# An unused 96-byte tile at the far end of SBUF, and a pool taken tile by tile, in a gated linear-attention and GEGLU kernel

## The chip, the cores and the metric

The kernel runs on one core of a Trainium2 chip. The metric is the device time of one execution in microseconds. Three runs of the kernel before took 2397.22, 2397.6 and 2398.0 us; their median, 2397.6 us, is the time before.

## The reference

For one sequence of 2048 tokens with 1024 features, in float32:

```python
g = sigmoid((x * gate_w).sum(-1, keepdims=True))
q, k, v = split_heads(x @ wqkv)                    # 32 heads of 32
phi = lambda t: concat(softmax(t @ w_phi), softmax(-(t @ w_phi)))
kv, z = phi(k).T @ v, phi(k).sum(tokens)           # per head
a = merge_heads((phi(q) @ kv) / (phi(q) @ z + 1e-6)) @ wo
b = (gelu(x @ w_gate) * (x @ w_up)) @ w_down       # 3584 hidden features
return g * a + (1 - g) * b
```

## The kernel before, in words

**Arithmetic.** Each float32 operand is split into a high and a low part (`split`, or `high` on ScalarE at L509 and `low` on VectorE at L512), both of type float32r, and each product is three matmuls: high by high, high by low, low by high (`PASSES`). Nearly all matmuls have a stationary tile of 128x128 and a moving tile of 128x512.

**Three stages**, one after the other on TensorE:

1. *Keys and values* (up to about 425 us). For two halves of the heads, 16 chunks of 128 tokens each: `keys_values` (L235) issues 48 matmuls `pd<-wkv,x` for a chunk. Their stationary operand is a slice of `x`, their moving operand the folded weight `wkv`. Behind them come the 8 matmuls `pg<-f,vs` (L271) of the chunk before, which accumulate the attention state. The features (softmaxes) of a chunk are made by VectorE and ScalarE meanwhile.
2. *Gate, up and query projections* (about 425 to 1698 us). A scheme with seven block products in place of eight computes two output blocks by two token blocks in 64 units. A unit is seven products of 12 matmuls each (`product`, L854): `a<-x,wgu`, `p<-s,tyz`, `c<-x,tyz` (of the unit before), `a<-s,tyz`, `a<-s,v` (of the unit before), `c<-x,wgu`, `b<-s,tyz`. The name after the arrow lists the moving and the stationary operand: the moving ones are the quarters `x` and the sums `s1` to `s4`, the stationary ones the weight slots `wgu`, `tyz` and `v`. In some units four more matmuls `misc<-pts,kbs` (L1085) do the attention of queries. The gated results `h` go out to the DRAM tiles `lm` by DMAs that POOL issues (`spill`, L139).
3. *Output* (about 1698 us to the end). The same kind of scheme: 126 steps of 24 matmuls (L1310, into `po`). The stationary operand of a step is a left block, made anew for each step in the slots `wgu`, `wgu`, `wl` by turns; the moving operand is a right block, made from `w_down` or `wo` and used twice or more, in one of ten slots by turns: three `tyz`, then seven `tw`. Right blocks are staged in four tiles `sr` (`load_rights`, L1223); left blocks in the tiles `stage`.

**Order.** In stages 2 and 3, and for PE and DVE in stage 1 too, the order of instructions on each engine and on the SP queue is the order in which the program writes them (`manual_schedule`). An engine or the queue whose next instruction waits does nothing else.

**Where the tiles lie.** All pools take their space per partition from the two ends of SBUF. From the low end, behind 16 KiB that are reserved and four small constants, come `keep`, `ring` (with `wgu`, `stage` and the quarters `x`), and above them in turn `kp` and `kl` (stage 1), `fa` and `fp` (stage 2, with `s3`, `s4`, `h` and `kbs`) and `op` (stage 3, with `sr`, `sl`, `wl`, `tw`). From the high end down come `kw` (stage 1, with `wkv`), and later `mid` (with `tyz`) and `xa` (with `s1`, `s2`, `v`, `pts`). The four small constants end at byte 16512, and `keep` takes 512 bytes, so `ring` begins at 17024, which is 128 modulo 256; every large tile of the low end is a multiple of 512 bytes long and begins at 128 modulo 256 (and modulo 512). The high end is at 229344, 32 bytes below 224 KiB, and the tiles there are multiples of 2 KiB long, so all of them begin at 224 modulo 256 (480 modulo 512). The gap between the two ends is 352 bytes where it is least.

**How space is handed on.** The first instruction that touches a tile of a new pool waits for the old users of that space. With the default of `tile_pool` it waits until the old pools there are done with as a whole; with `reuse_waits="tile"` (already set for `mid`, `xa`, `fa` and `fp`) it waits for those old tiles alone that lay under this tile. The pool `op` has the default.

Of the kernel before, what the change touches and what calls it, by code (L numbers as in the profile page):

```python
# [8 lines left out]
F32 = mybir.dt.float32  # L9
# [7 lines left out]
P = 128  # L17
# [9 lines left out]

LAG = 4


@with_exitstack
def tile_gated_mix(ctx: ExitStack, tc: tile.TileContext, x, xT, wkT, wqT, wv, w_phi, wo,
                   w_gate, w_up, w_down, gate_w, out):
    nc = tc.nc

    keep = ctx.enter_context(tc.tile_pool(name="keep", bufs=1))
    ring = ctx.enter_context(tc.tile_pool(name="ring", bufs=2))
    psum_a = ExitStack()
    psum_d, psum_g = (psum_a.enter_context(tc.tile_pool(name=n, bufs=1, space=PSUM)) for n in ("pd", "pg"))
# [118 lines left out]
    PE, DVE, ACT, SP = (getattr(mybir.EngineType, n) for n in ("PE", "DVE", "Activation", "SP"))  # L158
# [978 lines left out]


    fours = [ctx.enter_context(tc.tile_pool(name=f"po{n}", bufs=4, space=PSUM)) for n in range(2)]
    with tc.tile_pool(name="op", bufs=1) as op, tc.manual_schedule(engines={PE, DVE, ACT, SP}):  # L1140
        acc = [ring.tile([P, 4, D], F32, name=f"x{n // 2}{n % 2}", bufs=1) for n in range(4)]
        SLOTS, MID, STAGED = N_MLP, 3, 4

# [208 lines left out]
```

## Time and profile before

| | |
|---|---|
| median of three runs | 2397.6 us |
| the profiled execution: its time, its span | 2398.33 us, 2396.5 us |
| TensorE matmul busy, x instructions | 2390.1 us, x10601 |
| VectorE, ScalarE busy | 1806.0 us, 1053.9 us |
| moved by DMA | 448.70 MB, mean 187 GB/s |
| granted TensorE clock | 1.000 |

The profiled execution was taken by the hardware profiler. Its span runs from the first to the last instruction; its time is 1.83 us longer than the span, and 0.73 us longer than the median of the runs. Busy times of one engine are not additive with those of others, since the engines run beside each other. A matmul overlaps the next: each has a duration of nearly 0.4 us by its record, but the next one starts after some 0.23 us. What counts is therefore the spacing, which is read from the start of one group of matmuls to the start of the next, by the count of the first.

### The profile page before, as it was taken

Reading aid. Unit: us, or ns where it says so; the run is one execution under the profiler, and the core shown is the slowest. Engines: PE = TensorE matmul, PEld = TensorE weight load, DVE = VectorE, ACT = ScalarE, POOL = GpSimd, SP = SyncE. Lnnn points to the kernel's source line nnn. Section 1 sums busy time; section 2 is a strip of 40 time slices with the busy share of each in tenths; the row PEclk is TensorE's granted clock in tenths of the full one; section 3 lists DMA queues with packets and bytes.
Section 4 is the critical chain, followed back from the end, with each engine's and each line's share of the span. In section 5 each row is a group of like instructions: output and inputs, shape, how many; then the busy total and the mean of one; then the engine's idle time right before and its main releaser. Section 6 shows DMA issues by size and latency. Waiting matters only on the chain.

```text
span 2396.5 us, 28304 instructions
## 1 busy us (share of the span) xinstructions
PE 2390.1 (100%) x10601; PEld 1954.6 (82%) x10601; DVE 1806.0 (75%) x2354; ACT 1053.9 (44%) x1378; POOL 170.9 (7%) x318
## 2 busy tenths in 40 slices
PE   9999999999999999999999999999999999999999
PEld 7888888888888888888888888888788888888887
DVE  7987888788788777777888778784574868867773
ACT  4323322745545444455566655554433222323221
POOL 0000010111111111110000000000000000000000
PEclk9999999999999999999999999999999999999999
DMA  8322562644444565574444444433684767977873
GB/s 301 103 73 80 195 205 97 214 162 176 159 159 164 184 205 196 178 265 136 137 151 147 133 142 151 138 128 128 237 290 166 266 223 248 333 266 272 288 263 134
DMA packets 154906, 448.70 MB, mean 187 GB/s; under 512 B 21904, under 2 KB 21904, under 8 KB 153744
## 3 DMA queue, kind: packets, MB, share of 16 engines
q1 hardware_dynamic: 124256, 346.60, 43.5%
q0 software_dynamic: 29472, 100.16, 10.9%
q8 instruction: 83, 1.36, 0.3%
q14 instruction: 55, 0.45, 0.1%
q10 hardware_dynamic: 1040, 0.13, 0.0%
HBM read 337.25 MB, written 109.58 MB: 186 GB/s over the span
## 4 chain that ended last, share of the span: by engine, by line
PE 99%; DMA 1%; DVE 0%; issue 0%; ACT 0%; SPq 0%; ACTq 0%; DVEq 0%
PE po L1310 29%; PE a L854 22%; PE c L854 15%; PE pd L235 15%; PE b L854 7%; PE p L854 7%; PE pg L271 1%; PE misc L1085 1%; PE pd L144 0%; PE pd L225 0%; DMA early<-in_wkT 0%; PE pd L545 0%; PE pg L225 0%; DMA sr<-in_w_down 0%; DMA phi_c<-in_w_phi 0%; PE pg L545 0%
## 5 line engine op out<-in xcount | busy, mean ns | idle before, releaser
L235 PE MATMUL pd<-wkv,x 128*128 128x512 f32 x1536 | 366.7, 396 | 0.0
L235 PEld LDWEIGHTS pd<-wkv,x 128*128 128x128 f32 x1536 | 285.3, 188 | 66.0 <-DVE x L44 0.3
L1310 PE MATMUL po<-tw,wgu 128*128 128x512 f32 x1344 | 310.1, 389 | 0.0
L1310 PEld LDWEIGHTS po<-tw,wgu 128*128 128x128 f32 x1344 | 252.3, 188 | 52.7
L509 ACT ACTIVATE wgu<-stage 128x1024 fp32r<-128x1024 f32 x146 | 154.3, 1057 | 236.6 <-DVE stage L1200 159.5
L512 DVE TENSOR_TENSOR wgu<-stage,wgu 128x1024 fp32r<-128x1024 f32 x146 | 178.1, 1220 | 81.3 <-ACT wgu L509 79.9
L512 DVE TENSOR_TENSOR tyz<-stage,tyz 128x1024 fp32r<-128x1024 f32 x129 | 157.0, 1217 | 63.0 <-ACT tyz L509 62.9
L854 PE MATMUL c<-x,tyz 128*128 128x512 f32 x768 | 190.0, 396 | 0.0
L854 PE MATMUL a<-s,v 128*128 128x512 f32 x768 | 189.5, 395 | 0.0
L854 PE MATMUL b<-s,tyz 128*128 128x512 f32 x756 | 187.1, 396 | 0.0
L854 PE MATMUL a<-s,tyz 128*128 128x512 f32 x768 | 185.5, 390 | 0.0
L854 PE MATMUL p<-s,tyz 128*128 128x512 f32 x756 | 184.7, 393 | 0.0
L854 PE MATMUL c<-x,wgu 128*128 128x512 f32 x756 | 183.6, 391 | 0.0
L854 PE MATMUL a<-x,wgu 128*128 128x512 f32 x756 | 182.5, 390 | 0.0
L854 PEld LDWEIGHTS c<-x,tyz 128*128 128x128 f32 x768 | 144.5, 188 | 34.2
L854 PEld LDWEIGHTS a<-s,v 128*128 128x128 f32 x768 | 144.5, 188 | 34.0
L854 PEld LDWEIGHTS a<-s,tyz 128*128 128x128 f32 x768 | 144.0, 188 | 32.1 <-DVE tyz L512 0.6
L854 PEld LDWEIGHTS b<-s,tyz 128*128 128x128 f32 x756 | 142.2, 188 | 33.9
L854 PEld LDWEIGHTS p<-s,tyz 128*128 128x128 f32 x756 | 141.9, 188 | 32.6
L854 PEld LDWEIGHTS c<-x,wgu 128*128 128x128 f32 x756 | 142.0, 188 | 32.0
L854 PEld LDWEIGHTS a<-x,wgu 128*128 128x128 f32 x756 | 141.9, 188 | 31.0
L1310 PE MATMUL po<-tyz,wgu 128*128 128x512 f32 x672 | 160.2, 396 | 0.7 <-DVE wgu L512 0.7
(199 smaller groups left out, 3460.6 us busy)
## 6 DMA issues: line engine op xcount, KB each, us to landing
stage<-lm SPq DMA_DIRECT2D x98, 512.0 KB, 4.5
sr<-in_w_down SPq DMA_DIRECT2D x84, 512.0 KB, 4.7
sl<-lm SPq DMA_DIRECT2D x70, 512.0 KB, 4.6
lm<-h POOLq DMA_DIRECT2D x112, 256.0 KB, 2.4
stage<-in_w_gate SPq DMA_DIRECT2D x43, 512.0 KB, 3.8
stage<-in_w_up SPq DMA_DIRECT2D x43, 512.0 KB, 3.7
tg<-stage POOLq DMA_DIRECT2D x28, 512.0 KB, 3.0
tu<-stage POOLq DMA_DIRECT2D x28, 512.0 KB, 2.9
```

What stands on the lines that cost most here:

```text
L235: nc.tensor.matmul(ps[m], xb[b, kc // 4][:, a, kc % 4, t * P:(t + 1) * P], w[:, e, m * 512:(m + 1) * 512], start=kc == 0 and i == 0, stop= ...
L271: nc.tensor.matmul(pkv[d // 2][:, d % 2], vs[:, d].rearrange("p a b -> p (a b)"), f[:, :, :, heads], start=first and d % 2 == 0, stop=last ...
L509: nc.scalar.activation(dst, src, AF.Copy)
L512: nc.vector.tensor_tensor(dst, src, dst_h.bitcast(F32), OP.subtract)
L854: nc.tensor.matmul(dst, w[:, h, 4 * part + kc, :], xq[:, e, kc, :], start=first and kc == 0 and i == 0, stop=kc == 3 and i == 2, skip_grou ...
L1085: nc.tensor.matmul(po[p], kbs[:, p].rearrange("p a b -> p (a b)"), pts[:, q, p, :], start=q == 0, stop=q == 1)
L1310: nc.tensor.matmul(ps[c], lefts[s][:, a, m, c * P:(c + 1) * P], made[k][:, e, m], start=d == 0 and m == 0 and n == 0, stop=d == n_duo - 1 ...
```

## The change

A new pool `edge` with one tile of 24 float32 (96 bytes per partition) is opened at the high end of SBUF before all others, and the tile is never written or read. All tiles of `kw`, `mid` and `xa` so lie 96 bytes lower: they begin at 128 modulo 256, as those of the low end do (modulo 512 they begin at 384, those of the low end at 128). And the output stage's pool `op` gets `reuse_waits="tile"`. No instruction is added, removed or moved in its engine's order by the source.

```diff
@@ -27,6 +27,8 @@
 
 LAG = 4
 
+EDGE = 24
+
 
@@ -34,6 +36,8 @@
     nc = tc.nc
 
     keep = ctx.enter_context(tc.tile_pool(name="keep", bufs=1))
+    edge = ctx.enter_context(tc.tile_pool(name="edge", bufs=1, side="right"))
+    edge.tile([P, EDGE], F32, name="edge")
     ring = ctx.enter_context(tc.tile_pool(name="ring", bufs=2))
@@ -1137,7 +1141,7 @@
 
     fours = [ctx.enter_context(tc.tile_pool(name=f"po{n}", bufs=4, space=PSUM)) for n in range(2)]
-    with tc.tile_pool(name="op", bufs=1) as op, tc.manual_schedule(engines={PE, DVE, ACT, SP}):
+    with tc.tile_pool(name="op", bufs=1, reuse_waits="tile") as op, tc.manual_schedule(engines={PE, DVE, ACT, SP}):
         acc = [ring.tile([P, 4, D], F32, name=f"x{n // 2}{n % 2}", bufs=1) for n in range(4)]
         SLOTS, MID, STAGED = N_MLP, 3, 4
```

## The prediction

> **What bounds the kernel now.** I read the page first: the busy times, the row of the granted clock and the chain that ended last.
>
> ```profile
> span 2396.5 us, 28304 instructions
> ...
> PE 2390.1 (100%) x10601; PEld 1954.6 (82%) x10601; DVE 1806.0 (75%) x2354; ACT 1053.9 (44%) x1378; POOL 170.9 (7%) x318
> ...
> PEclk9999999999999999999999999999999999999999
> ...
> PE 99%; DMA 1%; DVE 0%; issue 0%; ACT 0%; SPq 0%; ACTq 0%; DVEq 0%
> ```
>
> TensorE is busy for the whole span, its clock is granted in full in every slice, and the chain is matmuls for 99%. So the time is the number of matmuls by their spacing, and only two things can shorten it: fewer pauses or a smaller spacing. The view of waits, for TensorE alone, says how much pauses can give:
>
> ```profile
> PE pd L192 <- DVE ones L181: 1.1, 1, 1.1
> PE po L1310 <- DVE wgu L512: 0.7, 1, 0.7
> ```
>
> These are the two longest of four lines; the second is the stage boundary treated below. Pauses are thus at most 1.1 and three times 0.7 us, 3.2 in all. The spacing remains. I read it from the timeline of TensorE, as the start of one group to the start of the next, by the count of the first (columns: start, duration, line, out<-moving,stationary, count). First the output stage, where the moving operand changes between the slots `tw` (low end) and `tyz` (high end):
>
> ```profile
> 1749.47 11.04 PE L1310 MATMUL po<-tw,wgu 128*128 128x512 f32 x48
> 1760.35 5.78 PE L1310 MATMUL po<-tyz,wl 128*128 128x512 f32 x24
> 1765.96 11.08 PE L1310 MATMUL po<-tw,wgu 128*128 128x512 f32 x48
> 1776.88 5.60 PE L1310 MATMUL po<-tw,wl 128*128 128x512 f32 x24
> ```
>
> 1749.47 to 1760.35 is 10.88 us for 48 matmuls, 226.7 ns each. Then `tyz` comes: 5.61 us for 24, 233.8 ns. Then `tw` again: 10.92 us for 48. Same shapes, type, clock, line and PSUM pool; what differs is where the moving tile lies. Both `tw` and the left slots begin at 128 modulo 256; `tyz` begins at 224. The same in the projections:
>
> ```profile
> 652.19 1.10 PE L1085 MATMUL misc<-pts,kbs 128*128 128x512 f32 x4
> 653.13 2.93 PE L854 MATMUL c<-x,wgu 128*128 128x512 f32 x12
> ...
> 658.71 2.90 PE L854 MATMUL a<-x,wgu 128*128 128x512 f32 x12
> 661.44 2.93 PE L854 MATMUL p<-s,tyz 128*128 128x512 f32 x12
> 664.21 2.97 PE L854 MATMUL c<-x,tyz 128*128 128x512 f32 x12
> 667.01 2.90 PE L854 MATMUL a<-s,tyz 128*128 128x512 f32 x12
> 669.75 2.96 PE L854 MATMUL a<-s,v 128*128 128x512 f32 x12
> 672.55 2.91 PE L854 MATMUL c<-x,wgu 128*128 128x512 f32 x12
> 675.29 2.97 PE L854 MATMUL b<-s,tyz 128*128 128x512 f32 x12
> 678.10 2.89 PE L854 MATMUL a<-x,wgu 128*128 128x512 f32 x12
> ```
>
> The seven products of a unit, 12 matmuls each, take 2.73 (`a<-x,wgu`, 128 against 128), 2.77 (`p<-s,tyz`, 224 against 224), 2.80 (`c<-x,tyz`, unlike), 2.74 (`a<-s,tyz`, 224 against 224), 2.80 (`a<-s,v`, unlike), 2.74 (`c<-x,wgu`, 128 against 128) and 2.81 us (`b<-s,tyz`, unlike). 12 by 226.7 ns would be 2.72. So it isn't the place of one operand that costs, since 224 against 224 comes within 0.02 us of the floor, but that the two operands of a matmul differ modulo 256. An alike product behind an unlike one first needs some matmuls to fall into step: 2.73 to 2.77 in place of 2.72. And in the first stage:
>
> ```profile
> 109.21 11.35 PE L235 MATMUL pd<-wkv,x 128*128 128x512 f32 x48
> 120.40 1.12 PE L271 MATMUL pg<-f,vs 128*128 128x256 f32 x8
> 121.36 11.35 PE L235 MATMUL pd<-wkv,x 128*128 128x512 f32 x48
> ```
>
> 11.19 us for 48 matmuls `pd<-wkv,x` (224 against 128), 233.1 ns; then 0.96 us for the eight shorter ones.
>
> **The change part by part, and the sum.** It adds no instruction. The address shift makes the two operands of every matmul alike modulo 256, at 128. I take the spacing that like operands have in the long runs of `tw`, 226.7 ns, for all matmuls with 512 columns. The counts:
>
> ```profile
> L235 PE MATMUL pd<-wkv,x 128*128 128x512 f32 x1536 | 366.7, 396 | 0.0
> ...
> L854 PE MATMUL c<-x,tyz 128*128 128x512 f32 x768 | 190.0, 396 | 0.0
> ...
> L1310 PE MATMUL po<-tyz,wgu 128*128 128x512 f32 x672 | 160.2, 396 | 0.7 <-DVE wgu L512 0.7
> ```
>
> ```profile
> L1310 PE MATMUL po<-tyz,wl 128*128 128x512 f32 x336 | 80.8, 395 | 0.0
> ...
> L1085 PE MATMUL misc<-pts,kbs 128*128 128x512 f32 x128 | 35.1, 396 | 0.0
> ```
>
> Stage 1: 1536 matmuls are 32 chunks of 48; a chunk falls from 11.19 to 10.88 us: 32 by 0.31 is 9.9 us. Stage 2: 768 is 64 units of 12; a unit of 84 falls from 19.39 (658.71 to 678.10) to 19.04 us: 64 by 0.35 is 22.4. The 128 attention matmuls go in fours, 0.94 us for four against 0.91: 32 by 0.03 is 1.0. Stage 3: 672 and 336 are 42 steps with `tyz`, from 5.61 to 5.44: 42 by 0.17 is 7.1; and the 0.04 us of falling into step behind about 12 blocks of `tyz` steps, 0.5. Together 40.9 us, all of it on the path, since nothing else ends a wait there.
>
> The other edit is worth a pause at the stage boundary (all engines, same columns):
>
> ```profile
> 1690.11 2.97 PE L854 MATMUL b<-s,tyz 128*128 128x512 f32 x12
> ...
> 1692.92 2.97 PE L854 MATMUL a<-s,v 128*128 128x512 f32 x12
> ...
> 1695.81 1.06 ACT L509 ACTIVATE tyz<-stage 128x1024 fp32r<-128x1024 f32 x1 [1.33 <-DVE stage L1113]
> ...
> 1702.18 0.54 POOL L139 DMA_DIRECT2D lm<-h  x1 [1.91 <-DVE h L836]
> 1706.86 1.92 SPq L1223 DMA_DIRECT2D sr<-in_w_down  x4
> 1707.01 1.06 ACT L509 ACTIVATE wl<-stage 128x1024 fp32r<-128x1024 f32 x1 [10.14 <-DMA lm<-h]
> ...
> 1715.38 0.73 PE L1310 MATMUL po<-tyz,wgu 128*128 128x512 f32 x2
> ...
> 1716.83 11.00 PE L1310 MATMUL po<-tyz,wgu 128*128 128x512 f32 x46 [0.71 <-DVE wgu L512]
> ```
>
> ScalarE's cast into `wl` and the SP queue's four loads into `sr` stood ready and waited until 1707, for the landing of the last `h` store, issued at 1702.18: `op` asked for the whole of the old pools. ScalarE sat 10.14 us behind that, with the casts of the next right and left blocks queued behind it on ScalarE, the loads of `lm` behind the `sr` loads on SP, VectorE waiting for both; so the left block of the step at 1715.38 came late and two matmuls took 1.45 us in place of 0.45. Tile by tile, `wl` waits only for the last reader of `s4` (`a<-s,v`, over at 1695.9) and `sr` for that of `s3` (`b<-s,tyz`, over at 1693.1). So `wl` can start when ScalarE has done its `tyz` cast (1695.81 plus 1.06), 10 us earlier, and the `sr` loads some 13 us earlier. That removes 1.0 us. If this cover were gone, the pause would grow by what the 72 matmuls before it save, 72 by 6.6 ns, to 1.5 us. Next late there are the `lm` loads behind the last `h` store, which no step needs before its tenth. The `sr` loads, 2 MB, now collide with the last stores; I cost that at nothing, the stores being consumed only then, and at 1 us at most.
>
> What must come off: the first two chunks run while weights are still being loaded and folded, so that a faster matmul only waits longer: 0.6 us. Falling into step behind the folds of stage 1 (16 of them), at the 0.05 us that `p<-s,tyz` shows: 0.8 us; the bounds are 0 and 2.3 us (the 30 entries behind `pg<-f,vs` as well). And new waits for the engines that feed TensorE:
>
> ```profile
> 60.00:80.00 20.00, 20.00 (x94) 16.42 (x93) 18.76 (x24) 6.70 (x9) 0.00 (x0) 1.00 0.37 129
> 480.00:540.00 60.00, 60.00 (x262) 48.84 (x261) 53.13 (x79) 29.07 (x40) 7.57 (x14) 1.00 0.45 159
> 2040.00:2100.00 60.00, 60.00 (x264) 49.22 (x263) 49.22 (x49) 18.45 (x18) 3.79 (x7) 1.00 0.93 332
> ```
>
> VectorE is busy for 94% of 60 to 80 us, 88.5% of 480 to 540, 82% of 2040 to 2100. A chunk of 12.15 us shrinks to 11.84; VectorE's work in it, 0.938 by 12.15 or 11.4 us, still fits. A unit shrinks by 1.8%, which makes 88.5% into 90%. DMA goes from 0.93 to 0.94 of its time. So TensorE stays the bound everywhere, and what comes back is a few single waits. No row prices them: 0 at least, and at most some 5 us (a quarter of a unit's gain in every unit). I take 1.0, nearer to 0, because the two views above show hardly a wait now.
>
> Sum: 40.9 plus 1.0 minus 0.6, 0.8 and 1.0 is 39.5 us. The profiled execution's own time is 2398.3 us, its span 2396.5; its time would be 2358.8. It stands 0.7 us above the median of the runs, 2397.6, so the median would be 2358.
>
> The doubt is how far the rows carry. In the trace the distance of like operands is always a multiple of 512 bytes; of unlike ones it is 352, 160 or 96 modulo 512. After the change tiles of the high end stand 256 modulo 512 from those of the low end, a distance that no row shows. Bounds from the rows: 226.7 ns if it counts as like, 233 to 235 if as unlike (2.81 us for 12, and 0.94 for four, are the slowest), and 240 as an outer one, twice the excess. I take 226.7: what the unlike distances have in common is that they are no multiple of 64 bytes, and it is short blocks of that kind, not 512 bytes, that I hold the likelier unit.
>
> [...]
>
> **The rivals.**
>
> *No change: the unit is 512 bytes (or it isn't the address at all).* Then pairs of one end stay alike, pairs of both ends (stage 1, three of seven products, the `tyz` steps) stay unlike at some 233 to 234 ns, and only the boundary's 1.0 us is won: 2396.6. For it: no row shows 256. Against: nothing beyond the argument on 64 bytes; as for "not the address", the spacing changes exactly with the slot, four rows in a row. [...]
>
> *Half: the step is lost at every change of product.* `p<-s,tyz` is alike and still takes 2.77, behind a product that is also alike but at another place. If after the change each of the 448 products costs 2.77, a unit stays at 19.39 and stage 2 gives nothing; the other stages keep 9.9, 7.6 and 1.0 less 1.4 to 2.4: 2381. Against it: in the output stage the 48 matmuls at 1749.47 span two steps with other slots on both sides and lose nothing.
>
> *Slower: 256 is the worst distance.* If the cost rises with the distance up to half of 512, the 4,976 matmuls between the two ends (1536; three products of 64 units, 2304; 1008; 128) would go from some 233.7 to 240 ns: plus 31 us, less 1.0: 2428. It decides from any spacing above 233.7 ns for `pd<-wkv,x`. Against: the three unlike distances in the trace, 352, 160 and 96, all lie between 233 and 235, with no such trend.
>
> **How the numbers follow.** The forecast (all alike, feeders keep up) I give 0.72, with 2353 to 2366 as its own range: 2353 if nothing comes off and every pause goes, 2366 with the upper bounds of feeders and falling into step. Half, or something between: 0.10. No change: 0.12. Slower: 0.06. The likeliest gives 2358. A range of 2353 to 2382 holds the forecast and most of the half case, 0.8. About 0.2%, 4.8 us, is what a measurement of this kernel can tell from no change; so faster has 0.82, the same 0.12, slower 0.06.
>
> **What would show it right or wrong.** In the timeline after: 48 matmuls `pd<-wkv,x` in 10.9 us from start to start (right) or 11.2 (no change); the seven products at 2.72 each, a unit 19.04; `tyz` steps at 5.44 like those of `tw`. Near the boundary, a load into `sr` and the cast into `wl` some 10 us ahead of where they were against the last `misc` or `v` product, and no matmul group of the output stage with a wait for VectorE. VectorE's busy time unchanged, its share of the span one or two points higher. Wrong would be: like spacings as now (the unit is 512), alike products at 2.77 (falling into step each time), or matmul spacing at 226.7 with new waits on `tyz`, `wgu` or `pd` that eat it, in the view of waits.

## The result, and the profile after

The changed kernel takes 2357.12 us (median of five runs, 2356.58 to 2358.54) against 2398.0 us for the kernel before in five runs (2397.22 to 2399.34). The ratio is 0.9831, with a 95% interval of 0.9816 to 0.9845. The forecast was 2358, with 2353 to 2382 as its range. Ratios and intervals, here and below, leave out two executions of e1 that ran far longer than all others (4527.27 and 11812.12 us).

The page of the changed kernel: same matmuls, a span 41.7 us shorter, TensorE still busy throughout and now the whole of the chain that ended last.

```profile
span 2354.8 us, 28301 instructions
...
PE 2349.5 (100%) x10601; PEld 1953.8 (83%) x10601; DVE 1805.1 (77%) x2354; ACT 1053.6 (45%) x1378; POOL 171.0 (7%) x318
...
PE 100%; DMA 0%; SPq 0%; DVE 0%; issue 0%
```

The view of waits, for TensorE alone, has only these two lines left, both from the start of the kernel; the wait at the stage boundary is gone:

```profile
PE pd L196 <- DVE ones L185: 1.1, 1, 1.1
PE pg L229 <- DMA early<-in_wkT: 0.5, 1, 0.5
```

The timeline of TensorE (start, duration, line, out<-moving,stationary, count; lines are four higher than before). First stage:

```profile
106.35 11.07 PE L239 MATMUL pd<-wkv,x 128*128 128x512 f32 x48
117.26 1.11 PE L275 MATMUL pg<-f,vs 128*128 128x256 f32 x8
```

106.35 to 117.26 is 10.91 us for 48 matmuls `pd<-wkv,x`, where it was 11.19. A unit of the projections:

```profile
644.70 2.88 PE L858 MATMUL a<-x,wgu 128*128 128x512 f32 x12
647.42 2.88 PE L858 MATMUL p<-s,tyz 128*128 128x512 f32 x12
650.14 2.88 PE L858 MATMUL c<-x,tyz 128*128 128x512 f32 x12
652.86 2.88 PE L858 MATMUL a<-s,tyz 128*128 128x512 f32 x12
...
663.74 2.88 PE L858 MATMUL a<-x,wgu 128*128 128x512 f32 x12
```

Each product takes 2.72 us, also `c<-x,tyz`, which took 2.80, and `p<-s,tyz`, which took 2.77; 644.70 to 663.74 is a unit of 84 matmuls in 19.04 us. The output stage:

```profile
1714.37 11.04 PE L1314 MATMUL po<-tw,wgu 128*128 128x512 f32 x48
1725.25 5.60 PE L1314 MATMUL po<-tyz,wl 128*128 128x512 f32 x24
1730.69 11.04 PE L1314 MATMUL po<-tw,wgu 128*128 128x512 f32 x48
1741.57 5.60 PE L1314 MATMUL po<-tw,wl 128*128 128x512 f32 x24
```

The `tyz` step takes 5.44 us, like a `tw` step, and the 48 matmuls behind it 10.88: the slots can no longer be told apart by their spacing. And the stage boundary, all engines:

```profile
1660.50 2.23 SPq L1227 DMA_DIRECT2D sr<-in_w_down  x4
...
1663.83 1.04 ACT L513 ACTIVATE wl<-stage 128x1024 fp32r<-128x1024 f32 x1
...
1665.41 11.04 PE L1314 MATMUL po<-tyz,wgu 128*128 128x512 f32 x48
...
1669.06 0.54 POOL L143 DMA_DIRECT2D lm<-h  x1 [1.92 <-DVE h L840]
...
1676.29 5.60 PE L1314 MATMUL po<-tyz,wl 128*128 128x512 f32 x24
...
1681.73 11.04 PE L1314 MATMUL po<-tyz,wgu 128*128 128x512 f32 x48
```

The four loads into `sr` are issued at 1660.50, 8.6 us ahead of the last `h` store (1669.06); before, they came 4.7 us behind it. ScalarE casts into `wl` straight behind its `tyz` cast, 5.2 us ahead of that store in place of 4.8 behind. Against the store the loads have thus moved by 13.2 us and the cast by 10.1, as forecast (13 and 10), and the steps follow each other without a pause (1676.29 to 1681.73 is 5.44 us for 24).

### The profile page after: what moved, and what is told of

Same layout as the page of the kernel before. It is cut to its first block, busy times and chain, and to the rows that moved or that the text cites. A ratio compares the mean times of both kernels' runs of the same rounds, so it can differ in the third digit from the quotient of the medians.

```text
span 2354.8 us, 28301 instructions
## 1 busy us (share of the span) xinstructions
PE 2349.5 (100%) x10601; PEld 1953.8 (83%) x10601; DVE 1805.1 (77%) x2354; ACT 1053.6 (45%) x1378; POOL 171.0 (7%) x318
## 4 chain that ended last, share of the span: by engine, by line
PE 100%; DMA 0%; SPq 0%; DVE 0%; issue 0%
PE po L1314 29%; PE a L858 22%; PE pd L239 15%; PE c L858 15%; PE b L858 7%; PE p L858 7%; PE pg L275 1%; PE misc L1089 1%; PE pd L148 0%; PE pd L229 0%; PE pg L229 0%; PE pd L549 0%; DMA early<-in_wkT 0%; PE pg L549 0%; PE misc L303 0%; PE pd L303 0%
## 5 line engine op out<-in xcount | busy, mean ns | idle before, releaser
L239 PE MATMUL pd<-wkv,x 128*128 128x512 f32 x1536 | 357.7, 390 | 0.0
L858 PE MATMUL c<-x,tyz 128*128 128x512 f32 x768 | 184.5, 389 | 0.0
L858 PE MATMUL a<-s,v 128*128 128x512 f32 x768 | 184.5, 389 | 0.0
L858 PE MATMUL b<-s,tyz 128*128 128x512 f32 x756 | 181.6, 389 | 0.0
L1314 PE MATMUL po<-tw,wl 128*128 128x512 f32 x672 | 156.9, 389 | 0.0
```

The source lines that it names most:

```text
L239: nc.tensor.matmul(ps[m], xb[b, kc // 4][:, a, kc % 4, t * P:(t + 1) * P], w[:, e, m * 512:(m + 1) * 512], start=kc == 0 and i == 0, stop= ...
L858: nc.tensor.matmul(dst, w[:, h, 4 * part + kc, :], xq[:, e, kc, :], start=first and kc == 0 and i == 0, stop=kc == 3 and i == 2, skip_grou ...
L1314: nc.tensor.matmul(ps[c], lefts[s][:, a, m, c * P:(c + 1) * P], made[k][:, e, m], start=d == 0 and m == 0 and n == 0, stop=d == n_duo - 1 ...
```

## The experiments

The theory: the spacing of a float32r matmul stream depends on the byte distance modulo 256 between the moving and the stationary operand, and the change makes it 0 everywhere. The rivals: the output pool's edit gives a part of the gain; an operand's own place counts; the unit is another one.

**Each edit alone.** The pool's edit without the unused tile (e1), and the reverse (e2):

```diff
# e1, against the kernel before
-    with tc.tile_pool(name="op", bufs=1) as op, ...
+    with tc.tile_pool(name="op", bufs=1, reuse_waits="tile") as op, ...
# e2, against the changed kernel
-    with tc.tile_pool(name="op", bufs=1, reuse_waits="tile") as op, ...
+    with tc.tile_pool(name="op", bufs=1) as op, ...
```

> The output stage's pool taken tile by tile, without the 96-byte tile. Theory (the operands' relative place sets the spacing): all spacings as before, 11.19 us for 48 matmuls pd<-wkv,x and 5.6 us for a tyz step, and only the pause of 1.0 us at the stage boundary goes; time 2396 to 2397 us, about 0.04% less than before. Rival (the earlier start of the output stage feeds it better all along): some 5 us or more less than before.

Measured: 2397.0 us against 2397.69, ratio 0.9998 (0.9988 to 1.0008): no change that the times can tell. The timeline of e1 shows what it did: no pause any more (1714.80 to 1726.00 is 11.20 us for 48), and the spacing of before (1709.20 to 1714.80 is 5.60 for 24). The rival of an earlier feed all along is out.

```profile
1709.20 5.76 PE L1310 MATMUL po<-tyz,wl 128*128 128x512 f32 x24
1714.80 11.36 PE L1310 MATMUL po<-tyz,wgu 128*128 128x512 f32 x48
1726.00 4.27 PE L1310 MATMUL po<-tw,wl 128*128 128x512 f32 x18
```

> The 96-byte tile alone, the output stage's pool with its default. Theory: all spacings at 226.7 ns as in the changed kernel; the pause at the stage boundary comes back and is longer than the 1.0 us of before, about 1.5 us, since TensorE reaches the place earlier; time 2358.5 us, 40 us less than before. Rival (the two edits share the gain): 2365 us or more.

Measured: 2357.91 us, ratio 0.9836 (0.9822 to 0.9851), 0.8 us above the changed kernel's median. The pause is back:

```profile
1665.68 11.04 PE L1314 MATMUL po<-tyz,wgu 128*128 128x512 f32 x48
1676.57 5.60 PE L1314 MATMUL po<-tyz,wl 128*128 128x512 f32 x24
1682.15 0.73 PE L1314 MATMUL po<-tyz,wgu 128*128 128x512 f32 x2
1683.60 10.72 PE L1314 MATMUL po<-tyz,wgu 128*128 128x512 f32 x46 [0.72 <-DVE wgu L516]
```

Two matmuls take 1.45 us (1682.15 to 1683.60) in place of 0.45, and the 24 ahead of them 5.58 in place of 5.44: the pause is 1.1 us, little more than the 1.0 of before and not the 1.5 expected. The chain that it hangs on, all engines:

```profile
1669.33 0.54 POOL L143 DMA_DIRECT2D lm<-h  x1 [1.92 <-DVE h L840]
...
1673.90 1.06 ACT L513 ACTIVATE wl<-stage 128x1024 fp32r<-128x1024 f32 x1 [9.70 <-DMA lm<-h]
```

From the stage's first matmul to the last store it is 3.65 us, as before (3.64). But the cast into `wl` follows the store after 4.57 us where it was 4.83, and the matmuls go on 9.70 us behind the cast where it was 9.82: the chain is 0.4 us shorter, so the pause hardly grew. Whether that is the change's doing or the execution's, one trace of each can't tell. So the unused tile gives about 40 us by the times; what the pool's edit gives, 1 us, is read from the pause in the traces.

**The place itself.** All tiles alike, but at 224 (the 96 bytes at the low end, e3) and at 0 (e4):

```diff
# e3, against the changed kernel
-    edge = ctx.enter_context(tc.tile_pool(name="edge", bufs=1, side="right"))
-    edge.tile([P, EDGE], F32, name="edge")
+    low = ctx.enter_context(tc.tile_pool(name="low_edge", bufs=1))
+    low.tile([P, 24], F32, name="low_edge")
# e4, against the changed kernel
-EDGE = 24
+EDGE = 56
+    low = ctx.enter_context(tc.tile_pool(name="low_edge", bufs=1))
+    low.tile([P, 32], F32, name="low_edge")
```

> The 96 bytes are put at the low end, above the pool keep, in place of the high end: all large tiles begin at 224 modulo 256 in place of 128. Theory (only the distance of the two operands counts): 226.7 ns everywhere, time 2357 us as the changed kernel. Rival (the operand's own place counts, 128 being a good one): some or all products above 226.7 ns; if all went to the 233.3 ns of the unlike ones, 2425 us.

> Both ends are shifted (128 bytes at the low, 224 at the high end), so that all large tiles begin at 0 modulo 256. Theory (only the distance counts): 226.7 ns everywhere, 2357 us. [...]

Measured: 2356.93 us (ratio 0.9832, 0.9817 to 0.9846) and 2356.66 us (0.983, 0.9816 to 0.9845). First a row pair of e3's first stage, then one of e4's projections:

```profile
106.62 11.07 PE L239 MATMUL pd<-wkv,x 128*128 128x512 f32 x48
117.53 1.11 PE L275 MATMUL pg<-f,vs 128*128 128x256 f32 x8
```

```profile
658.20 2.88 PE L860 MATMUL c<-x,wgu 128*128 128x512 f32 x12
660.92 2.88 PE L860 MATMUL b<-s,tyz 128*128 128x512 f32 x12
```

10.91 us for 48 and 2.72 for 12, as in the changed kernel. The place does not count: for the whole kernel there is nothing special in 128, and nothing to win with 0.

**The distance.** Only the size of the unused tile differs:

```diff
-EDGE = 24
+EDGE = 8     # e5: 32 bytes, the high end at 192 modulo 256
+EDGE = 56    # e6: 224 bytes, at 0
+EDGE = 16    # e7: 64 bytes, at 160
+EDGE = 88    # e8: 352 bytes, at 128 modulo 512
```

> The unused tile has 32 bytes in place of 96: tiles of the high end begin at 192 modulo 256, 64 from those of the low end. Theory with a unit of 256 bytes: unlike, pairs of both ends at 233 to 235 ns, time 2390 to 2400 us. Rival with a unit of 64 bytes: like, 226.7 ns everywhere, 2357 us.

> The unused tile has 224 bytes: tiles of the high end begin at 0 modulo 256, 128 from those of the low end. Theory with a unit of 256 bytes: unlike, 2390 to 2400 us, and if the cost rises with the distance, 2400 to 2430. Rival with a unit of 64 or 128 bytes: 226.7 ns everywhere, 2357 us.

> The unused tile has 64 bytes: tiles of the high end begin at 160 modulo 256, 32 from those of the low end. Theory with a unit of 64 bytes or more: unlike, 233 to 235 ns between the ends, 2390 to 2400 us. Rival with a unit of 32 bytes is excluded by the kernel before (its distance of 352 is 11 times 32); a cost that rises with the distance would give less than the 96 of before: 2365 to 2390 us.

> The unused tile has 352 bytes, all that the gap holds: tiles of the high end begin at 128 modulo 512, like those of the low end. Theory with a unit of 256 bytes or less: as the changed kernel, 226.7 ns everywhere, 2357 us, since 256 is as good as 512. Rival (256 is better or worse than 512 in some hidden way): above or below 2357 by more than 3 us.

| run | distance of the high end from the low end, modulo 256 | median, us | ratio to before, interval |
|---|---|---|---|
| before | 96 | 2397.84 | 1 |
| e7 | 32 | 2395.48 | 0.9990 (0.9981 to 0.9999) |
| e5 | 64 | 2391.26 | 0.9973 (0.9962 to 0.9984) |
| e6 | 128 | 2392.54 | 0.9979 (0.9969 to 0.9989) |
| changed kernel (its own comparison) | 0 (256 modulo 512) | 2357.12 | 0.9831 (0.9816 to 0.9845) |
| e8 | 0 (0 modulo 512) | 2356.94 | 0.9829 (0.9814 to 0.9844) |

64 and 128 are unlike, so the unit is not 64 or 128 bytes; 256 is as good as 512. Nor does the cost rise with the distance. And one unlike distance can have more than one spacing. In e5 a step of the output stage, with the moving `tyz` 64 bytes (modulo 256) above the stationary slot, and then two chunks of the first stage, with the moving `wkv` 64 bytes above `x` too:

```profile
1757.08 5.67 PE L1314 MATMUL po<-tyz,wl 128*128 128x512 f32 x24
1762.59 11.09 PE L1314 MATMUL po<-tw,wgu 128*128 128x512 f32 x48
```

```profile
47.80 11.15 PE L239 MATMUL pd<-wkv,x 128*128 128x512 f32 x48
58.79 1.12 PE L275 MATMUL pg<-f,vs 128*128 128x256 f32 x8
59.74 11.37 PE L239 MATMUL pd<-wkv,x 128*128 128x512 f32 x48
70.95 1.12 PE L275 MATMUL pg<-f,vs 128*128 128x256 f32 x8
```

5.51 us for 24 is 229.6 ns. The chunk at 47.80 takes 10.99 us, 229.0 ns, and the next, at the same distance, 11.21 us, 233.5 ns. Of the 26 chunks that run in one piece four take 229.0 to 229.3 ns and the others about 233.4. So for unlike operands the distance alone does not set the spacing; what decides between the two is not shown. In the changed kernel all 26 take 227.2 or 227.3 ns, the first few matmuls included.

**The disputed cost by itself.** Two small kernels, each run once, hold nothing but groups of 96 matmuls on one tile of zeros (and a load, a memset and stores ahead of them). Shortened, their operands and groups are:

```python
def mov(d, k=0):  return big[:, 2048 * (k + 1) + d // 4:2048 * (k + 1) + d // 4 + 512]
def stat(d, k=0): return big[:, 512 * k + d // 4:512 * k + d // 4 + 128]
group("distg",      [(stat(0), mov(96))])                             # and other distances
group("own_like",   [(stat(0), mov(0)),     (stat(96, 1), mov(96, 1))])
group("own_unlike", [(stat(0), mov(96, 1)), (stat(96, 1), mov(0))])
group("stat_alt",   [(stat(0), mov(0)),     (stat(96, 1), mov(0))])   # e10
group("mov_alt",    [(stat(0), mov(0)),     (stat(0), mov(96, 1))])
group("far_like",   [(stat(0), mov(0)),     (stat(256, 1), mov(256, 1))])
```

> Nothing of the reference is computed here (the output is zeros): groups of 96 matmuls, stationary 128x128 and moving 128x512 of one tile of zeros, only the byte distance between the two differs; dista is 0, each further letter 16 bytes more (distc 32, diste 64, distg 96, disti 128, distk 160, distm 192, disto 224, distp 240, distq 256, dists 288). Theory (a unit of 256 bytes): 226.7 ns for 0 and 256, more for the others, 96 and 288 like 352 and 32 in the kernel. Two more groups alternate two operand pairs whose members lie 96 bytes apart. In own_like each matmul's own operands are alike and the stationary one of the next matmul is unlike to the moving one; in own_unlike it is the other way round. If what counts is the moving operand against the weights that are loaded beside it for the next matmul: own_like 230 ns or more and own_unlike 226.7. Rival, if a matmul's own two operands count: own_like 226.7, own_unlike 233.

From the timeline of e9; a spacing is the start of the next row less that of a row, by 96. The lines have the main pairs; the table below has every distance, read in the same way:

```profile
33.71 21.92 PE L37 MATMUL dista<-big 128*128 128x512 f32 x96
55.47 22.40 PE L37 MATMUL distb<-big 128*128 128x512 f32 x96
...
122.08 22.57 PE L37 MATMUL distg<-big 128*128 128x512 f32 x96
144.50 22.56 PE L37 MATMUL disti<-big 128*128 128x512 f32 x96
...
255.93 21.96 PE L37 MATMUL distq<-big 128*128 128x512 f32 x96
277.72 22.57 PE L37 MATMUL dists<-big 128*128 128x512 f32 x96
...
321.92 22.62 PE L37 MATMUL own_like<-big 128*128 128x512 f32 x96
344.38 22.27 PE L37 MATMUL own_unlike<-big 128*128 128x512 f32 x96
366.49 21.93 PE L37 MATMUL both_moved<-big 128*128 128x512 f32 x96
```

> Again nothing of the reference is computed (zeros out): groups of 96 matmuls at finer byte distances, named by 16-byte letter and 4-byte letter (distab 4, distac 8, distad 12, distbb 20, distda 48, distfa 80, distmc 200, distnb 212, distoa 224, distoc 232, distpb 244, distpd 252). If whole 16-byte pieces count, as 240 being as good as 0 suggests: 244 and 252 at 226.7 ns, and 4 to 12 either at 226.7 or at the 231.7 of 16. If only equality counts: all above 226.7. Three alternations: far_like takes two places 256 bytes and more apart, all pairs alike (226.7 if only the place modulo 256 counts); stat_alt moves only the stationary operand by 96 from matmul to matmul, mov_alt only the moving one. If a change costs as much as the mean of its two distances: 230 to 230.5 ns each; if a change of place costs by itself: more than that.

Of e10, the dearest distance, 244, with the row behind it:

```profile
258.85 23.20 PE L37 MATMUL distpb<-big 128*128 128x512 f32 x96
281.89 21.95 PE L37 MATMUL distpd<-big 128*128 128x512 f32 x96
```

The spacings at all distances of both:

| moving start above stationary start, bytes | ns per matmul |
|---|---|
| 0; 240; 252; 256 | 226.7; 226.8; 226.9; 227.0 |
| 12; 64 | 228.9; 228.9 |
| 80; 16 | 231.1; 231.7 |
| 8; 32; 48; 96; 128; 192; 200; 224; 232; 288 | 233.2 to 233.5 |
| 160 | 234.2 |
| 4; 212 | 236.7; 238.5 |
| 20; 244 | 240.0; 240.0 |

With no other engine at work the two spacings of the kernel appear, 226.7 at 0 and 227.0 at 256, 233.5 at 96. So the theory stands where the kernel uses it: with all operands at one place modulo 256, every long stream of the changed kernel (24 matmuls or more) and of these two runs comes to 226.7 to 227.9 ns, but for the first group of each small run (`warm`, 252.7 and 256.1). For the other distances the table has one stream each, and by e5 another stream at the same distance can settle elsewhere. That 288 is like 32 says little, since ten distances lie within 0.3 ns; e5 says more, where `tyz` stands 320 bytes modulo 512 above its slot, and in a long step the starts come 226, 229 and 232 ns apart by turns, as they do at 64 here. Why a given distance costs what it does is open. "Only equality" is wrong (240 and 252 are as good as 0), and so is "whole 16-byte pieces" (244 is, with 20, the worst).

The alternations don't settle which two operands matter to each other either. `own_like` takes 234.0 ns, though every matmul's own operands are alike: that is about the mean, 233.9, of the distances 96 and 160 which each moving operand has to the stationary one of the *next* matmul. But `own_unlike`, alike in that sense, takes 230.3 and 230.1, not 226.7. `stat_alt` and `mov_alt` take 230.0 and 230.1, about the mean of an alike and an unlike distance. `far_like` takes 226.7. What the streams bear out is only the case that the kernel has: all operands at one place modulo 256, 226.7 to 227.9 ns.

## Why the prediction was right

**The bound.** TensorE is the bound before and after; the time fell by the spacing and one pause, as forecast.

**The terms.** The first rows of stages 2 and 3, before and then after (that of stage 3 after, 1665.41, stands above):

```profile
425.01 3.02 PE L854 MATMUL a<-x,wgu 128*128 128x512 f32 x12
...
1698.54 11.36 PE L1310 MATMUL po<-tyz,wgu 128*128 128x512 f32 x48
```

```profile
415.41 3.01 PE L858 MATMUL a<-x,wgu 128*128 128x512 f32 x12
```

Stages 2 and 3 begin, by these, at 425.01 and 1698.54 before and at 415.41 and 1665.41 after. Stage 1 fell by 9.6 us (forecast: 9.9 less 0.6 and 0.8). Stage 2 fell from 1273.5 to 1250.0, by 23.5 (22.4 and 1.0, less the waits). Stage 3, to the end of the span, from 698.0 to 689.4, by 8.6 (7.1, 0.5 and 1.0). Together 41.7 in the profiled spans against 39.5; by the medians, 40.9. The two differ because the profiled execution before stands 0.3 us above its median of five and the one after 0.5 below.

**What was mis-sized: what was to come off, 2.4 us.** By the medians 1.0 of the 41.9 us came off, by the profiled spans 0.2. Two misses in stage 1 offset each other. From the start of the fourth chunk on (48.48 before, 47.05 after), each of 29 chunks gains 0.28 us and not 0.31: behind `pg<-f,vs` it takes 10.91 where the floor is 10.88. That falling into step, 0.9 us in all, stood in the prediction only as an upper bound. The first three chunks, on the other hand, gain 1.4 us where 0.3 was expected (three times 0.31 less 0.6); 0.4 of it is that TensorE's waits for the first loads and for `bd` are 0.9 us before and 0.5 after, and in two other runs of the kernel they are 0.7 (e1) and 0.2 (e2). And the feeders held. Of the changed kernel, a window, and VectorE's row that begins a chunk's features:

```profile
60.00:80.00 20.00, 20.00 (x94) 16.70 (x93) 19.79 (x25) 5.92 (x7) 0.00 (x0) 1.00 0.31 104
```

```profile
60.70 0.68 DVE L249 TENSOR_REDUCE mm<-pd 128x16 f32<-128x512 f32 x1
...
71.14 0.68 DVE L249 TENSOR_REDUCE mm<-pd 128x16 f32<-128x512 f32 x1
```

VectorE is busy for 19.79 of 20 us, 99%, where I had 96% from the shrunk chunk. But the share of a window is not the work of a chunk: VectorE does one chunk's work in 10.44 us here (60.70 to 71.14), as it did before, and not in the 11.4 that I had; a chunk of TensorE takes 11.86. It is busy throughout because it is working off a backlog. TensorE's waits show no line for this place.

**What was right for a wrong reason.** The step from "96, 160 and 352 are unlike" to "256 will be alike" rested on the guess that multiples of 64 bytes are alike. e5 and e6 refute the guess: 64 and 128 are not. 256 is; that it came so was luck on the ground given. The chance of 0.12 for no change was in its place, and the ground given for the 0.72 was not. Nor is it so that no row had 256: both tiles of `pg<-f,vs` begin at 128 modulo 512, and from one of its eight matmuls to the next the moving start goes up by 256 bytes and the stationary one by 512, so every second one stands at 256 modulo 512. From the third on they start 120 ns apart in most of the groups, without a difference between the two kinds. But no unlike pair with 256 columns was there to compare, so these rows could not have decided it.

**The boundary.** The pause of 1.0 us was read rightly, its mechanism too (e1 and e2). That it would grow to 1.5 us without its cover is wrong: it came to 1.1 in e2.

**The range.** The 2366 at the upper end of the forecast's own range does not follow from its terms: 2397.6 less 41.9, plus 0.6, 2.3 and 5, is 2363.6. The stated range of 2353 to 2382 does not rest on it.

**The rivals.** No change: a unit of 512 bytes is refuted by the time itself, and "not the address" by e5 to e8, which differ from the changed kernel in the size of the unused tile alone. Half: `p<-s,tyz` at 2.72 shows that what it lost before was the change of place modulo 256 against the product ahead, and not the change of tile. Slower: no trend with the distance, as the table shows; the most that a stream of one distance cost is 240.0 ns, the outer bound, at 20 and 244 bytes.

**The relative place alone.** e9 has 226.7 ns at 0 and 233.5 at 96 bytes with nothing but TensorE at work: for this stream the relative place costs 6.8 ns per matmul. What stands behind it, no run shows.

## What to carry to other kernels

Where TensorE is busy throughout, look at the spacing of its matmuls by tile, not by line: two spacings for one shape are worth a question, and where the tiles lie is a candidate that costs next to nothing to change (96 bytes here). In a float32r stream with new weights for each matmul (x10601 loads beside x10601 matmuls here), 128x128 against 128x512, put all operands at one place modulo 256 bytes; here that alone was worth 1.6% (e2). Other types and shapes were not tried. A pool that waits for whole old pools showed here as a ScalarE that stood ready for 10.14 us, until the last store of the stage before had landed: let such a pool wait tile by tile, and expect only what the pause itself costs, 1.0 us here.

## What the runs showed of the hardware that was not expected

- The spacing fell into a fixed pattern and kept it: in e9 the group `like`, behind an unlike one, has its first seven starts 240, 225, 230, 236, 229, 232 and 231 ns apart, and then 226 or 227 to its end. At an unlike distance the pattern was not the same each time: in e5 chunks with operands 64 bytes apart keep to 229 or to 233 ns.
- 226.7 ns is the least that any long 128x512 stream came to, also with all tiles at 0 modulo 256 (e4: 12 matmuls in 2.72 us). What sets it, no run shows.
- A distance of 20 bytes cost 13.3 ns per matmul, 12 bytes 2.2, and 4 bytes below an equal place 0.2, each in one stream of e10.
